# A hand-ordered attention-and-gated-MLP kernel: one written order of all steps replaced by another

## The chip, the cores and the metric

The kernel runs on one core of a Trainium2 chip. The time is the device time of one execution in microseconds (us). The core has five engines with a queue each: TensorE (PE, matrix products), VectorE (DVE), ScalarE (ACT), GpSimd (POOL) and SyncE (SP, which here issues every DMA).

## The reference

Inputs are q, k, v (4 batches, 8 heads, 768 positions, 64 wide), 8 memory keys and values per head, and five weights of an MLP.

```python
for c in range(24):                      # chunks of 32 positions
    k_ctx = k[:, :, max(0, 32*c-16) : min(768, 32*c+40)]   # v_ctx likewise
    scores = q_c @ concat(mem_k, k_ctx).T / 8
    out_c = softmax(scores) @ concat(mem_v, v_ctx)
x = out as (4, 768, 512)
h = gelu_tanh(x @ w_in)                  # 1024 wide
u, v = h[..., :512], h[..., 512:]
v_n = (v - mean(v)) / sqrt(var(v) + 1e-6) * g_ln
v_s = einsum('ts,bsd->btd', w_sg, v_n) + b_sg
result = x + (u * v_s) @ w_out
```

## The kernel before, in words

The kernel holds every operand of the MLP products as a high and a low part, and each product is three products (low x high, high x low, high x high) accumulated in PSUM. All work is cut into some 1230 named steps. The text `ORDER` (line 35) lists the names; the loop at line 565 walks through it and emits each step into its engine's queue. Every engine works its own queue strictly in that order, so `ORDER` is the schedule. A star after a name takes the second engine that the step may use. Buffers are handed out by `Slots` in the order of the text: four PSUM tiles (mma to mmd), two tiles `g` for the gelu of the v half, seven tiles `u`.

The steps, with u for a unit of 128 positions (24 units, six to each batch b), tt for a unit in its batch, h for a half batch (384 positions), j for a group of 128 columns:

- `r`, `d1` to `d6` with `i13` and so on: one 128x512 piece of w_in arrives as 64-bit words (512 KB) and is split into high and low. `r` loads (SP), `d1` ACT (star POOL), `d2` DVE (star ACT), `d3` and `d4` DVE, `d5` ACT, `d6` POOL (star DVE). `ri10` to `ri13` are the four pieces for the v half, `ri00` to `ri03` those for the u half; `ro0` to `ro3` the same for w_out, through one staging tile.
- `g`, `ga`, `gb`: one 128x384 piece of w_sg is loaded into a `u` tile (SP, 192 KB), its high part written by ACT, its low part by POOL (star DVE). Twelve pieces; those that end in 0 serve half 0.
- `q`, `k`, `v` and a unit: loads of 256, 368 and 512 KB (SP).
- Attention of a unit: `S` scores (PE), `mx` maxima and `sb` subtraction (DVE), `ex` exponentials (ACT), `z` clears missing keys (POOL, first and last unit of a batch), `sm` sums and `sr` reciprocals (DVE), `nm` scaling (DVE, star POOL). For units 0 to 9 `T` transposes on PE and `p` copies back (ACT, star DVE); later pairs of units use `yt` (DVE) and four exchanges `Ea` to `Ed` of four small DMAs each. `A` multiplies by the values (PE), `xc` and `xh` copy out and round (ACT), `xl` makes the low part (POOL, star DVE; units 0, 2, 4, 5 always DVE).
- `V` and b, tt: the product with the v half of w_in (PE, 12 matmuls of 512 columns). `v1` to `v4` gelu (ACT, DVE, ACT, DVE), `v5`, `vx` statistics (DVE), `vy`, `v6` the inverse deviation (POOL), `v7` normalization (DVE, star POOL), `v8` high part (ACT), `v9` low part (POOL, star DVE) into the tiles `vh`.
- `U` and b, h, j: the product with the u half (12 matmuls of 384 columns), `u1` to `u4` gelu (ACT, DVE, ACT, DVE).
- `W`: the product of the six `vh` with w_sg (18 matmuls of 384 columns), `w1` scale and shift and `w2` gate (DVE), `w3` high (ACT), `w4` low (POOL, star DVE).
- `O`: the product with w_out (12 matmuls), `o1` adds x (DVE), `out` stores (SP).
- `zz` and a number: so many products of a cleared tile into the first free PSUM tile (function `warm`), whose results nobody reads.

A DMA that loads into a buffer waits on SP until the buffer's last reader is done, and all later DMAs wait behind it. q and k have two buffers each, v three.

The queues in words up to the first `W` of batch 0. SP before: ri13 k0 ri10 g40 g01 q0 g50 g21 g31 ri12 q1 k1 ri11 v0 ri02 q2 ri01 k2 v1 g20 q3 k3 ri00 v2 cb q4 k4 v3 ri03 v4 q5 g41 k5 ro0 and so on. PE before: zz25 S0 zz15 S1 zz3 T0 zz4 A0 zz2 T1 zz5 S2 V00 A1 S3 T2 V01 A2 S4 T3 V02 A3 T4 S5 A4 V03 V04 U003 T5 U000 S6 A5 U002 V05 U012 T6 S7 A6 U010 S8 U011 U001 T7 S9 U013 A7 S10 W011.

Of the kernel before, what the change touches and what calls it, by code (L numbers as in the profile page):

```python
# [40 lines left out]
g41 d3i00 p2 k5 sb3 cbh v500 ex3 vx00 sm3 ro0 A2 v101 sr3 vy00 d4i00 S4 v201 nm3* xh2 v5 d5i00 xl2 q6 v600 xc2  # L41
T3 mx4 d6i00 V02 v301 sb4 k6 p3 d1i03 v401 v700* ex4 v501 sm4 A3 vx01 sr4 d2i03 v800 nm4 xc3 v6 v900* T4 xh3
d3i03 S5 p4 xl3* vy01 v102 v601 A4 mx5 q7 v701* d2o0* k7 v202 V03 xh4 v7 sb5 xc4 xl4 ex5 d3o0 v801 d4i03 v302
v901* d5i03 V04 v402 z5 v103 d6i03 sm5 v203 ga50 sr5 v502 v303 nm5* U003 ga21 v403 ga40 gb21 vx02 ga31 v503
ga20 vx03 vy02 ga01 g30 gb50* T5 ga41 gb20* U000 g11 p5 gb41* g00 gb01* u1003 gb40* g10 u2003 vy03 g51 v602 S6
u3003 gb31 ga30 A5 u4003 q8 ga11 mx6 k8 v702* u1000 U002 v8 sb6 xh5 xc5 u2000 ex6 xl5 v603 ga00 u3000 gb11*
V05 v802 v703 u1002 u4000 z6 v902 ga10 sm6 ga51 u2002 v803 gb10 sr6 v104 U012 u3002 v204 nm6* u4002 v304 v903*
T6 v404 gb00 v105 S7 p6 v504 gb51 u1012 A6 v205 q9 k9 mx7 v305 U010 v9 vx04 xc6 u2012 vy04 v604 v405 u3012
v704* sb7 u4012 ex7 S8 v505 u1010 sm7 U011 k10 v804 q10 u2010 sr7 v904 vx05 u3010 mx8 u4010 U001 nm7 d1o0 sb8
vy05 u1011 ro1 v605 u2011 ex8 v705 u3011 T7 sm8 v805 S9 p7* v905 U013 u4011 k11 mx9 q11 sr8 sb9 d1o1 nm8 A7  # L50
ex9 d4o0 sm9 d2o1* S10 v10 gb30* xc7 sr9 W011 d5o0 d3o1 q12 k12 u1001 mx10 ro2 d4o1 u2001 d5o1 sb10 u3001
d6o1* ex10 W002 w1011 sm10 w2011 sr10 u4001 w3011 d6o0* S11 d2o2* w4011* w1002 d1o2 W000 q13 d3o2 u1013 k13
mx11 ro3 u2013 w2002 u3013 d4o2 w3002 u4013 d5o2 W003 w4002* w1000 d6o2* w2000 w3000 d2o3 w4000 W012 w1003
w2003 d1o3* w3003 d3o3 W010 w4003 w1012 w2012 d4o3 w3012 w4012 d5o3 d6o3 T8 w1010 W013 p8 w2010 nm9 w3010
w4010 sb11 ex11 z11 T9 sm11 A8 p9 nm10* w1013 sr11 w2013 S12 xc8 v11 yt10 w3013 A9 q14 mx12 nm11* k14 sb12
W001 v12 w4013 yt11 ex12 Ec5 z12 sm12 sr12 nm12 O012 w1001 Eb5 w2001 w3001 w4001* S13 o1012 Ea5 O002 mx13 sb13
ex13 q15 O013 sm13 out012 o1002 Ed5 sr13 S14 o1013 O011 mx14 k16 out002 sb14 out013 q16 ex14 k15 O003 sm14
o1011 yt12 out011 sr14 nm13* O001 o1003 out003 yt13 nm14 O000 o1001 out001 S15 o1000 xh6 xh7 out000 O010 xl6
mx15 q17 xh8 xl7* k17 sb15 xl8* ex15 V10 o1010 sm15 out010 xc9 sr15 xh9 xl9* U100 v110 v210 v310 U103 v410
u1100 u2100 v510 u3100 u4100 V13 u1103 vx10 vy10 u2103 v610 u3103 v710 u4103 v810 v910* U101 v113 v213 v313  # L60
V12 v413 u1101 u2101 v513 u3101 u4101 vx13 vy13 V11 v613 v112 v713 v212 v813 v312 v913 v412 A10 v512 v111 v211
S16 xc10 v13 vx12 v311 A11 vy12 mx16 q18 v612 xh10 k18 v411 U102 xc11 Ec6 xl10* xh11 v511 v712 sb16 v812 V14
v14 vx11 u1102 xl11* v912 Ed6 ex16 u2102 sm16 u3102 vy11 v611 u4102 sr16 v711* V15 v114 Ea6 v214 v314 v811
v414 Eb6 S17 v911 v514 vx14 U110 mx17 vy14 v115 v614 v215 k19 v714 v315 q19 U113 v814 v415 u1110 v914 v515
u2110 vx15 U111 u3110 yt14 vy15 v615 u1113 u4110 nm15 u2113 A12 sb17 u1111 u3113 v715 ex17 S18 u4113 v15 v815
u2111 z17 U112 k20 xc12 mx18 q20 u3111 v915* yt15 sm17 W110 nm16 sr17 sb18 u4111 ex18 z18 sm18 S19 w1110 sr18
A13 mx19 k21 q21 w2110 W111 xc13 Eb7 w3110 w4110 u1112 Ea7 u2112 W100 u3112 w1111 u4112 w2111 v16 w3111 Ed7
w4111 W113 w1100 w2100 Ec7 w3100 w4100* W112 w1113 w2113 w3113 w4113* W103 w1112 yt16 w2112 nm17 w3112 w4112*
sb19 W102 w1103 ex19 yt17 w2103 nm18* sm19 w3103 sr19 w4103 S20 w1102 w2102 A14 q22 mx20 k22 w3102 W101 sb20
w4102 xc14 v17 ex20 sm20 sr20 O110 w1101 w2101 w3101 w4101 O111 o1110 out110 O103 o1111 out111 O102 o1103  # L70
out103 O100 o1102 out102 O112 o1100 out100 A15 o1112 out112 S21 Ec8 O101 mx21 k23 v18 O113 o1101 xh12 Ea8 xh14
xl12* xh13 xl14 xl13* V20 o1113 out101 Eb8 U201 v120 v220 out113 xc15 Ed8 v320 V22 xh15 v420 u1201 xl15* u2201
q23 v520 u3201 u4201 V21 v122 vx20 vy20 v222 v620 v720* v322 yt18 v422 V23 v522 v820 nm19 vx22 v920* yt19 vy22
v121 v622 U200 sb21 v722* v221 ex21 v321 sm21 A16 v421 u1200 v822 nm20 S22 u2200 xc16 v19 v922* u3200 A17 xh16
v521 v123 u4200 xl16 U202 Ed9 xc17 vx21 v223 xh17 mx22 vy21 v323 v621 sr21 sb22 xl17 V24 v423 u1202 Eb9 ex22
u2202 v721 u3202 sm22 v821 u4202 v921 Ea9 sr22 V25 v523 vx23 vy23 v124 v623 v224 v723 v20 v324 Ec9 U213 v823
v424 v923 v524 vx24 U211 vy24 v125 v624 u1213 v225 v724* u2213 v325 u3213 U210 v425 u1211 u4213 v824 yt20 v924
v525 A18 u1210 u2211 u2210 nm21* u3211 S23 vx25 v21 xc18 u4211 u3210 vy25 yt21 A19 v625 mx23 U212 xc19 Ec10
nm22 sb23 v725 ex23 u4210 v825 z23 U203 sm23 Ea10 u1212 v925 u2212 sr23 u3212 u4212 W203 Eb10 v22 W213 w1203
Ed10 W202 w1213 w2213 w3213 w4213* yt22 u1203 A20 u2203 nm23* w1202 u3203 w2202 W211 xc20 v23 yt23 w3202 u4203  # L80
w4202* w2203 w3203 w4203 A21 w1211 w2211 W212 Eb11 w3211 w4211* Ea11 W200 w1212 w2212 w3212 Ec11 w4212* W201
w1200 w2200 Ed11 w3200 w4200* W210 w1201 w2201 w3201 w4201 O200 w1210 w2210 w3210 w4210 O201 o1200 out200 O213
o1201 out201 O212 o1213 out213 O211 o1212 out212 O203 o1211 out211 O202 o1203 out203 O210 o1202 xh18 xh20
out202 xl18* xh19 xl20 V30 o1210 xl19 out210 xc21 xh21 V31 v130 xl21* v230 v330 v430 V33 v131 v530 v231 vx30
v331 vy30 v630 v431 U302 v730* v531 vx31 A22 vy31 v830 v631 u1302 v930* U301 xc22 u2302 v731* v133 u3302 v233
xh22 u4302 v333 A23 xl22* v831 v433 u1301 V32 xc23 v931* xh23 u2301 v533 u3301 xl23* u4301 vx33 U312 v132 vy33
v633 v232 v733 v332 V35 v833 v432 u1312 v933 v532 u2312 vx32 u3312 vy32 v632 u4312 V34 v135 v732* v235 v335
v435 v832 U303 v535 v932 vx35 vy35 v134 v635 U310 v234 u1303 v735* u2303 v334 u3303 v434 U311 u4303 u1310 v534
v835 u2310 v935* u3310 U313 vx34 u1311 u4310 vy34 v634 u2311 v734 u3311 v834 u4311 U300 u1313 v934 u2313 u3313
u4313 W313 W301 w1313 w2313 w3313 w4313* u1300 u2300 W311 w1301 u3300 w2301 u4300 w3301 w4301* W312 w1311  # L90
# [543 lines left out]
```

## Time and profile before

| | us |
|---|---|
| median of 3 runs (lowest, highest) | 390.04 (387.78, 390.69) |
| the profiled execution, its own time | 390.77 |
| its span, first to last instruction | 388.7 |
| busy: PE, DVE, ACT, POOL | 375.4, 259.5, 157.0, 127.3 |

All times of the trace are counted from the span's start. PE's busy time includes the `zz` products. The granted clock is TensorE's, as a share of 2.4 GHz.

### The profile page before, as it was taken

How to read it: one execution, taken by the hardware profiler on the slowest of the kernel's cores; microseconds unless marked ns; L12 is line 12 of the kernel's file. 1: busy time of each engine (PE TensorE's matmuls, PEld its weight loads, DVE VectorE, ACT ScalarE, POOL GpSimd, SP SyncE). 2: the span in 40 equal slices, each digit the busy share in tenths (PEclk: the TensorE clock that was granted, in tenths of full speed). 3: DMA queues.
4: the chain of work that ended last, by engine and by line, in shares of the span. 5: the costliest groups of instructions: out<-in, count | busy, mean ns of one | idle time of the engine just before them, and what ended most of it. 6: DMA issues, size and time to landing. Idle time of an engine off the chain costs nothing.

```text
span 388.7 us, 11100 instructions
## 1 busy us (share of the span) xinstructions
PE 375.4 (97%) x4798; PEld 345.5 (89%) x4798; DVE 259.5 (67%) x476; ACT 157.0 (40%) x291; POOL 127.3 (33%) x142
## 2 busy tenths in 40 slices
...
GB/s 289 398 387 288 239 142 123 240 218 147 1 201 131 262 1 57 162 166 119 95 102 84 121 135 77 70 110 95 73 39 81 83 0 2 3 0 2 0 81 83
DMA packets 24529, 47.65 MB, mean 123 GB/s; under 512 B 4384, under 2 KB 13600, under 8 KB 24480
## 3 DMA queue, kind: packets, MB, share of 16 engines
...
q14 instruction: 11, 0.09, 0.1%
HBM read 36.96 MB, written 6.29 MB: 111 GB/s over the span
## 4 chain that ended last, share of the span: by engine, by line
PE 74%; DVE 10%; SPq 4%; DMA 4%; ACT 3%; issue 2%; POOL 2%; DVEq 0%; POOLq 0%; ACTq 0%
PE mma L105 18%; PE mmd L105 17%; PE mmb L105 16%; PE mmc L105 14%; PE av L105 5%; SPq L105 4%; PE s L105 3%; DMA ka<-in_ks 2%; DMA kb<-in_ks 1%; DMA pt<-y 1%; DVE na L105 1%; DVE w_sg_lo L105 1%; DVE ga L105 1%; ACT ea L105 1%; DVE rdc L105 1%
## 5 line engine op out<-in xcount | busy, mean ns | idle before, releaser
L105 DVE SCALAR_TENSOR_TENSOR mmd<-mmd,g_half,b_half 128x384 f32<-128x384 f32 x11 | 6.9, 624 | 14.4 <-PE mmd L105 14.4
L105 PE MATMUL mma<-vhf 128*128 128x512 f32 x43 | 13.4, 474 | 2.3 <-POOL vhf L105 2.3
L105 PEld LDWEIGHTS mma<-vhf 128*128 128x128 f32 x43 | 9.8, 235 | 4.8 <-POOL vhf L105 2.3
L105 POOL TENSOR_SCALAR rsa<-mva 128x1 f32<-128x1 f32 x8 | 2.0, 248 | 36.0 <-DVE mva L105 36.0
L105 PE MATMUL mmc<-w_in_hi,paira 128*128 128x512 f32 x48 | 13.4, 401 | 0.1
L105 DVE STREAM_TRANSPOSE y<-na 128x512 f32<-128x512 f32 x14 | 9.9, 707 | 3.8 <-DMA pt<-y 2.9
L105 ACT ACTIVATE ea<-ea 128x512 f32<-128x512 f32 x12 | 7.6, 635 | 11.1 <-DVE ea L105 11.0
L105 ACT ACTIVATE eb<-eb 128x512 f32<-128x512 f32 x12 | 7.6, 635 | 11.1 <-DVE eb L105 11.0
L105 PEld LDWEIGHTS s<-kb,qb 64*32 64x32 f32 x768 | 8.4, 105 | 3.8 <-DVE xa L105 1.8
L105 PE MATMUL s<-kb,qb 64*32 64x64 f32 x768 | 10.3, 224 | 1.5 <-DMA kb<-in_ks 1.5
L105 DVE SCALAR_TENSOR_TENSOR gb<-gb,mma 128x512 f32<-128x512 f32 x10 | 6.9, 686 | 6.9 <-ACT gb L105 6.9
L105 PE MATMUL s<-ka,qa 64*32 64x64 f32 x768 | 10.3, 224 | 0.7 <-DVE eb L105 0.7
L105 PEld LDWEIGHTS av<-pt,va 64*64 64x64 f32 x512 | 8.3, 134 | 2.9 <-ACT pt L105 1.4
L105 PEld LDWEIGHTS s<-ka,qa 64*32 64x32 f32 x768 | 8.4, 105 | 2.7 <-issue 1.1
L105 PEld LDWEIGHTS mmc<-w_in_hi,paira 128*128 128x128 f32 x48 | 8.7, 188 | 2.1 <-DVE paira L105 0.3
L105 PEld LDWEIGHTS av<-pt,vc 64*64 64x64 f32 x512 | 8.5, 134 | 2.3 <-issue 0.9
L105 PE MATMUL av<-pt,vc 64*64 64x32 f32 x512 | 9.4, 221 | 0.7 <-ACT xc L105 0.7
L105 PEld LDWEIGHTS av<-pt,vb 64*64 64x64 f32 x512 | 8.4, 134 | 1.8 <-issue 1.1
L105 PE MATMUL av<-pt,va 64*64 64x32 f32 x512 | 9.2, 220 | 0.8 <-ACT pt L105 0.8
L105 ACT ACTIVATE ga<-ga 128x512 f32<-128x512 f32 x12 | 7.6, 634 | 5.6 <-DVE ga L105 5.5
L105 DVE SCALAR_TENSOR_TENSOR ga<-ga,mmc 128x512 f32<-128x512 f32 x12 | 8.2, 681 | 2.3 <-ACT ga L105 2.3
L105 DVE SCALAR_TENSOR_TENSOR mma<-mma,g_half,b_half 128x384 f32<-128x384 f32 x7 | 4.4, 625 | 7.5 <-PE mma L105 7.5
(535 smaller groups left out, 1249.7 us busy)
## 6 DMA issues: line engine op xcount, KB each, us to landing
...
pt<-y SPq DMA_DIRECT2D x112, 32.0 KB, 2.3
...
```

The costliest lines, as they stand in the source:

```text
L105: return self.tc.keep_in_program_order(getattr(self.engine, name)(*args, **kw))
```

## The change

Only the text `ORDER` changes. It holds the same steps as before, in another order; 85 of them change their engine (among those on DVE before and POOL now: `nm1`, `nm2`, `nm7`, `nm9`, `nm17`, `nm19`, `nm22`; from POOL to DVE `nm0`, `nm10`, `nm21`, `nm23`). DVE gets 464 steps in place of 476, ACT 295 for 290, POOL 138 for 131. The `zz` products go from 54 to 39 and stand at other places. Below are the old text up to the first `W` and the new text up to there and at the places that the prediction names.

```diff
-ri13 k0 ri10 g40 g01 q0 g50 g21 d2i13* d1i13* g31 ri12 d3i13 d4i13 d2i10* q1 d1i10* d5i13 k1 ri11 d3i10 zz25
-S0 v0 d6i13* ri02 d4i10 q2 mx0 d5i10 ri01 sb0 d6i10 ex0 k2 d2i12* z0 sm0 d1i12 v1 d3i12 zz15 S1 g20 sr0 d4i12
-nm0* mx1 d5i12 q3 d1i11 sb1 zz3 T0 d2i11 ex1 d6i12* p0 sm1 zz4 A0 k3 d3i11 sr1 d4i11 d1i02 ri00 nm1 xc0 v2
-d2i02 zz2 T1 xh0 d3i02 d5i11 xl0 cb d2i01* d6i11 d1i01 zz5 S2 p1 d3i01 V00 mx2 q4 k4 d4i01 sb2 v3 d5i01 d4i02
-ex2 d6i01 d5i02 sm2 A1 v100 sr2 ri03 nm2 S3 xc1 v200 d6i02 xh1 T2 v4 mx3 v300 xl1* d2i00* q5 v400 d1i00 V01
...
+ri13 d2i13 d1i13 d3i13 d4i13 d5i13 zz4 zz6 zz2 q0 k0 d6i13 ri12 S0 zz13 zz3 zz7 mx0 sb0 ri10 d2i12* d1i12
+d3i12 d4i12 ex0 z0 d2i10* ri11 d5i12 d1i10 d2i11* d1i11 sm0 d3i10 sr0 nm0 T0 k1 q1 S1 v0 d4i10 d3i11 d6i12*
+d4i11 q2 k2 ri01 k3 q3 ri00 v1 mx1 sb1 p0 d5i10 A0 d5i11 xh0 ex1 xl0 d6i11* d6i10 S2 sm1 sr1 mx2 sb2 V00
+d2i01* d1i01 ex2 d3i01 d4i01 sm2 S3 mx3 sr2 nm1* T1 nm2* sb3 v100 xc0 v200 d2i00* p1 zz3 A1 T2 zz1 d3i00 v2
+ri02 ex3 v300 xc1 xh1 d1i00 p2 sm3 sr3 v400 v500 vx00 nm3* T3 A2 d2i02* vy00 v600 xl1* d4i00 V01 xc2 d1i02
+v700 v800 xh2 p3 d3i02 d4i02 xl2 v101 k4 v3 q4 cb ri03 v4 d5i00 v201 v900 cbh d6i00 S4 k5 q5 k6 g11 g10 g40 q6
+g21 A3 V02 mx4 sb4 d5i02 d6i02* d2i03* v301 v401 v501 xc3 xh3 d5i01 d1i03 xl3* d3i03 vx01 d4i03 S5 V03 g30 q7
+mx5 d6i01* sb5 S6 d5i03 d6i03 U001 v102 ex4 v202 sm4 v302 ga10 ga30 vy01 v601 gb10 sr4 nm4 T4 v402 v701 mx6
+sb6 ga40 ga11 ga21 p4 u1001 gb40 gb21 v801 ex6 ex5 z6 z5 v502 vx02 u2001 sm5 U002 k7 S7 A4 ro0 g20 g50 g51 k8
+g31 q9 q8 v5 k9 v6 d2o0* u3001 u4001 gb11 xh4 u1002 ga20 xc4 mx7 sr5 xl4 v901 nm5* vy02 u2002 v103 v203 sm6
+sr6 u3002 ga50 gb20 v602 U003 u4002 sb7 v702 V04 ga31 u1003 v303 u2003 v403 v503 T5 p5 v802 S8 mx8 vx03 nm6*
+A5 ga51 ex7 xh5 xl5 sm7 sr7 gb30* sb8 v902 T6 U000 xc5 p6 u3003 u1000 v104 V05 vy03 gb50* gb31 nm7* v603 gb51
+k10 v7 u4003 ex8 v204 v304 sm8 v703 v404 S9 A6 T7 v504 sr8 mx9 g41 g00 v803 ga41 p7 gb41* u2000 nm8 vx04 q10
+v903 g01 v105 ga00 ga01 vy04 q11 k11 v8 U012 U011 u3000 xc6 v205 sb9 ex9 sm9 u4000 u1011 v305 v405 u2011 S10
+mx10 v505 A7 vx05 v604 v704* gb01 gb00 T8 p8 v804 xc7 u3011 U013 U010 vy05 v605 v705 u1012 v805 u1010 v905
+d1o0 v904* A8 sb10 u4011 S11 d3o0 u2012 u2010 u3010 W001 u3012 sr9 u4010 nm9* mx11 u4012 W002 W003 sb11 d4o0
...
+nm15 sb17 o1012 xh9 xh10 xh11 v811 xl9* q18 out011 S18 v13 out013 k20 vy10 xl10* mx18 xl11* yt15 V13 out010
...
+V15 U112 V14 xc12 v115 v215 v315 vy13 v613 v713 u1112 u1110 v415 v515 vx15 v813 vy15 u2112 u2110 v913* ex18
+v114 v214 v314 A13 S19 mx19 v414 v514 vx14 v615 v715* v815 u3112 u4112 U111 u1111 xc13 u3110 z18 v915* vy14
+v614 U113 U100 v714 u4110 u1113 v814 v914* u2113 u3113 u4113 W110 w1110 u2111 u3111 w2110 Ed7 q20 k21 Ea7 Ec7
...
+U203 v19 v18 Eb9 out111 out113 Ea9 Ec9 k23 q23 out110 Ed9 vy23 v623 sr21 v422 u2200 u2201 u3200 u3201 v522
+v723* v823 v923 u1203 xl17* u4201 mx22 u2203 vx22 vy22 v622 v722* V24 v124 u3203 u4200 v224 u4203 v324 v424
+sb22 v524 vx24 U213 V25 U210 U212 A18 v822 v922* vy24 v624 v724* v125 v225 v325 v425 u1213 v525 yt20 u2213
...
+out301 out211 out212 out210 o1300 o1313 out312 out313 out300 O310 o1310 out310 O302 o1302 out302
```

## Rows read from the trace of the kernel before

**Rows 1.** The page: busy us, share of the span, instructions, by engine.
```profile
PE 375.4 (97%) x4798; PEld 345.5 (89%) x4798; DVE 259.5 (67%) x476; ACT 157.0 (40%) x291; POOL 127.3 (33%) x142
```

**Rows 2.** Windows: us, length, busy PE, PEld, DVE, ACT, POOL, PE clock, DMA share, GB/s.
```profile
0.00:10.00 10.00, 7.65 (x22) 6.04 (x23) 2.69 (x5) 3.14 (x4) 4.77 (x12) 1.00 0.82 293
...
20.00:30.00 10.00, 8.82 (x226) 6.56 (x219) 9.71 (x15) 6.75 (x13) 5.67 (x5) 1.00 1.05 388
...
11.87:85.59 73.72, 69.07 (x1401) 57.73 (x1402) 68.29 (x125) 51.15 (x97) 41.21 (x39) 0.98 0.71 249
...
82.10:385.30 303.20, 300.30 (x3334) 283.89 (x3328) 190.90 (x354) 104.71 (x195) 80.74 (x91) 1.00 0.28 87
```

**Rows 3.** PE in order of time, 0 to 83 us: start, length, tile, [idle before].
```profile
2.35 8.70 PE L105 MATMUL mma<-vhf 128*128 128x512 f32 x25 [2.35 <-POOL vhf L105]
10.98 0.86 PE L105 MATMUL s<-ka,qa 64*32 64x64 f32 x64
...
23.80 1.20 PE L105 MATMUL mmc<-w_in_hi,paira 128*128 128x512 f32 x4
...
31.18 1.31 PE L105 MATMUL mma<-w_in_hi,paira 128*128 128x512 f32 x4 [1.14 <-DVE paira L105]
...
35.70 1.14 PE L105 MATMUL av<-pt,vc 64*64 64x32 f32 x64
36.77 0.86 PE L105 MATMUL s<-ka,qa 64*32 64x64 f32 x64
37.55 0.66 PE L105 MATMUL mmb<-ident,na 128*128 128x128 f32 x4
...
48.22 1.09 PE L105 MATMUL mma<-w_in_hi,pairb 128*128 128x512 f32 x4
...
51.02 0.86 PE L105 MATMUL mmd<-paira,w_in_lo 128*128 128x384 f32 x4
...
53.11 0.60 PE L105 MATMUL mmc<-ident,na 128*128 128x128 f32 x4
53.46 0.94 PE L105 MATMUL mmb<-paira,w_in_lo 128*128 128x384 f32 x4
...
82.10 0.44 PE L105 MATMUL mmb<-w_sg_hi,vha 128*128 128x384 f32 x1
```

**Rows 4.** Windows of PE alone: us, length, busy PE, clock, DMA share, GB/s.
```profile
2.35:5.00 2.65, 2.65 (x6) 1.00 0.96 376
...
8.00:10.00 2.00, 2.00 (x10) 1.00 1.07 390
...
33.00:34.00 1.00, 1.00 (x4) 0.50 1.05 408
```

**Rows 5.** DVE in order of time.
```profile
11.87 0.69 DVE L105 TENSOR_REDUCE mxa<-s 128x8 f32<-128x512 f32 x1 [1.28 <-PE s L105]
...
22.19 0.68 DVE L105 TENSOR_TENSOR paira<-av,paira 128x512 fp32r<-128x512 f32 x1
...
27.55 1.78 DVE L105 TENSOR_TENSOR na<-ea,rdc 128x512 f32<-128x512 f32 x1
```

**Rows 6.** DMA issues on SP, 0 to 32 us, and in us to landing, rawc and y.
```profile
5.69 0.46 SPq L105 DMA_DIRECT2D rawc<-in_w_in  x1
...
DMA to landing us min/median/max: 6.8/6.8/6.8
...
31.07 0.43 SPq L105 DMA_DIRECT2D y<-in_w_out  x1
...
DMA to landing us min/median/max: 6.4/6.4/6.4
```

**Rows 7.** PE in order of time after 82 us: the longest idle time.
```profile
130.77 0.85 PE L105 MATMUL s<-kb,qb 64*32 64x64 f32 x64 [1.46 <-DMA kb<-in_ks]
```

**Rows 8.** POOL in order of time.
```profile
15.81 1.44 POOL L105 TENSOR_TENSOR na<-ea,rda 128x512 f32<-128x512 f32 x1 [1.59 <-DVE rda L105]
```

More of the change, by code (lines that the diff above doesn't have):

```diff
@@ L41 @@
[L41 to L90, printed above, removed]
@@ new lines @@
+k10 v7 u4003 ex8 v204 v304 sm8 v703 v404 S9 A6 T7 v504 sr8 mx9 g41 g00 v803 ga41 p7 gb41* u2000 nm8 vx04 q10
+v903 g01 v105 ga00 ga01 vy04 q11 k11 v8 U012 U011 u3000 xc6 v205 sb9 ex9 sm9 u4000 u1011 v305 v405 u2011 S10
+mx10 v505 A7 vx05 v604 v704* gb01 gb00 T8 p8 v804 xc7 u3011 U013 U010 vy05 v605 v705 u1012 v805 u1010 v905
+d1o0 v904* A8 sb10 u4011 S11 d3o0 u2012 u2010 u3010 W001 u3012 sr9 u4010 nm9* mx11 u4012 W002 W003 sb11 d4o0
+d5o0 ex10 w1001 w2001 w3001 ro1 d2o1* k12 v10 d1o1 d3o1 d4o1 d5o1 k13 v9 q13 q12 ex11 w1002 w4001 w2002 w1003
```

36 lines of the change are left out of this document (33 added, 3 removed).

## The prediction

> **What bounds the kernel now.** The page's first part comes first: PE is busy 97% of the span [rows 1], so time can only come from PE's own work or from stretches where PE idles, waits or spends itself on products that nobody reads. The windows show where these are. From 82.10 us to the last product PE idles 303.20 - 300.30 = 2.90 us in all [rows 2], 1.46 of it in front of one score product [rows 7]. Ahead of 82.10 the picture is another one. By then PE has done 11 S, 8 A, 8 T, 6 V and 8 U, in the order of the text. One S takes 0.78 us from its start to the next start, A 1.07, T 0.35, V 2.80, U 2.09 [rows 3]: 8.6 + 8.6 + 2.8 + 16.8 + 16.7 = 53.5 us. So 28 of the first 82 us are not needed by PE. In the first 10 us VectorE works 2.69 us, because it waits for data; from 11.87 (the first maximum, [rows 5]) to 85.59 (the first `w1`, right behind the first W) it is busy 68.29 of 73.72 us with 125 instructions, 93% [rows 2]. The DMA engines are full too in that time (share 1.05 at 20 to 30 us, [rows 2]). The start is bound by loads in the order in which SP issues them, and then by VectorE's queue; after 82 us PE bounds.
>
> **The loads.** SP's DMAs land in the order of issue, at one pace: rawc (`ri12`) lands at 5.69 + 6.8 = 12.5 us and y (`ro0`) at 31.07 + 6.4 = 37.5 [rows 6]. In the old SP queue 3,120 KB are issued up to and with `ri12`, 12,642 KB up to and with `ro0` (512 KB for r and v, 368 for k, 256 for q, 192 for g, 386 for `cb`). That is 9,522 KB in 25.0 us, 381 KB per us, and a byte count of X lands at 4.3 + X/381. The new queue puts the w_sg pieces, five of which stand before `ri12` now, behind `k6`, and moves q0 ahead of k0. Its counts: k0 1,136, ri12 1,648, ri10 2,160, ri11 2,672, q1 3,296, v0 3,808, k2 4,432, v1 6,592, v2 7,104. So they land at 7.3, 8.6, 10.0, 11.3, 13.0, 14.3, 15.9, 21.6 and 22.9; by the same rule the old ri11 (4,256) landed at 15.5 and v0 (4,768) at 16.8.
>
> **The warm-up products.** Of 54 there remain 39, 12 of them before S0 in place of 25. The first ones run at the lower clock level, 6 in 2.65 us or 0.44 each, those from 8 us on at the higher one, 10 in 2.0 us [rows 4] (the clock column reads 1.00 in both; I go by the pace). Twelve end at 2.35 + 12 x 0.43 = 7.5 us, when k0 is there, and S0 starts at 7.5 in place of 10.98 [rows 3]. The other 23 before T0 fill 8.4 to 13.4 at 0.22 each, inside the wait for `nm0`; they cost nothing unless T0 is ready sooner. The last 4 stand in waits as well.
>
> **To the first V.** I walk down VectorE's new queue, 0.60 us from one 512-wide instruction to the next and 0.70 where a result is waited for (one takes 0.69, [rows 5]): mx0 8.45, sb0, d3i12, d4i12, sm0 to 11.8, d3i10, sr0, nm0 to 13.2. `nm0` now runs on VectorE for 0.6 us in place of 1.44 on POOL, where it ended at 17.25 [rows 8]. T0 is at 13.3, p0 behind it, A0 at 14.5 (v0 landed at 14.3) until 15.5. VectorE goes on with d4i10, d3i11, d6i12, d4i11, mx1, sb1 to 16.9; ACT writes xh0 until 16.7, so xl0 ends at 17.5 (now 22.87, [rows 5]) and d6i11 at 18.1. V00 starts near 18.0; it starts at 23.80 now [rows 3]. **Gain at this point: 5.8 us.**
>
> **To the first W.** Two counts. The first walks down PE: from V00 to W001 stand 6 V, 8 U, 9 S, 8 A, 8 T, 16.8 + 16.7 + 7.0 + 8.6 + 2.8 = 51.9 us, 0.9 us of warm-ups and some 2.5 us where PE changes kind. With waits of about 1.2 in all around T1, T3 and A2 this gives 74.5. The second walks down VectorE: the new queue has 120 instructions between mx0 and `w1001`; at the present mean, 73.72/125 = 0.590 us with its idle time in it, w1001 comes at 8.45 + 70.8 = 79.2, so W001 starts 3.2 us before, at 76.0. The later of the two holds: 76.0. At that point the new order has done one S, one A and one T more than the old one at 82.10, so the point to compare is 82.10 + 2.2 = 84.3. **Gain: 8.3 us.** The w_sg pieces have become urgent in return: `g41`, `g00`, `g01` wait for `u` tiles that `gb50`, `gb31`, `gb51` free at 56 to 59.5 us, land by 64, and ACT splits them in front of `u3000`, `xc6` and `v305`; by my walk v905 ends at 73.5, 1 us before W001 is due. That cover is thin.
>
> **After the first W.** The same PE work remains, at the same pace, so 300.3 us of it stay. The present 2.90 us of idle could go; against it stand three places where I find a margin under 1 us: W110 (`V14`'s normalization has 8.1 us between V14 and W110), A18 (16 exchange DMAs and five more issues of 0.3 to 0.6 us each in 15 us), W311. I credit nothing. `out211`, `out212`, `out210` move behind `out301`: 11 stores in the last 10 us of PE, 192 KB or 0.5 us each at the pace above, so they still fit; exposed, they would cost 1 us. VectorE's 12 instructions fewer give nothing here, where it is idle a third of the time.
>
> **The sum.** 390.77 (the profiled execution) - 8.3 = 382.5. The median of the three runs is 390.04, 0.7 lower, so the forecast for a median is **381.7 us**, 2.1% faster. Its own bounds: 377.3, if the PE walk holds (9.9) and the 2.9 us go as well; 386, if W001 comes 4 us later than 76.
>
> **Rivals.** (1) *POOL and VectorE get in each other's way.* `nm1` to `nm3` stand on POOL in the densest stretch. One `na` on VectorE took 1.78 us where 0.69 is usual, at 27.55 us [rows 5], while POOL was at work. If each of the three costs VectorE 1.1 us: 381.7 + 3.3 = 385.0. Against it: in all POOL has hardly more to do before W (41 steps for 40, and three fewer of its longest, `v7`). The Trainium skill, SBUF — State Buffer, section Who interferes with whom, says that a VectorE instruction with two SBUF inputs contends with a GpSimd instruction that reads SBUF, and that the one issued second blocks until the first is done; the 1.78 us agree, and by that rule the moved `nm` are where the time would go.
>
> (2) *The clock falls more often.* Now V01 runs its products at 0.50 [rows 4], behind a wait of 1.14 us, and takes 35.70 - 31.18 = 4.52 us against V04's 2.80 [rows 3]: 1.7 us. The new order has 15 fillers less and between V00 (ends 20.4) and V01 (28.3) only 5 us of PE work. The forecast takes one such fall again. With two more: 381.7 + 3.4 = 385.1; then the fillers don't do what they are put there for. The Trainium skill, TensorE: Matmul & The Clock Gate, section Why this matters for your kernels, says to leave no long idle gaps of PE between bursts; by it the fewer fillers speak against the change, and the trace agrees as far as one fall goes.
>
> (3) *The early start is not kept.* VectorE may need 0.65 us for each of the 120 instructions: 0.06 x 120 = 7.2 us more to W001, 389 us, no change. For it: VectorE is the second bound and the new queue issues its steps earlier than the data of some of them. Against it: the 0.590 us already hold the waits of a queue that is as crowded, and the new one has fewer steps in it.
>
> (4) *Slower: ACT held by the late w_sg pieces.* ACT works in order; if `ga01` waits for its DMA, `u3000`, `xc6`, `ex9` and `v305` wait behind it, and v405 to v905 follow, 9 us from `ga01` to the end of v905. W001 is then at `g01`'s landing + 10. At 64 it is harmless; at 74.3 the whole gain is gone; from 78 on the kernel is slower by over 1%, at 80 it is 390.04 + 5.7 = 395.7. That needs `gb51` on POOL, and with it the load behind it, 14 to 16 us late. A load takes up to 6.8 us to land [rows 6], so two such loads in a row, each waiting for the tile that the other frees, would make it.
>
> **Chances.** Forecast 0.52; better than it, near 377.3, 0.10; rivals 1 and 2, 0.18 together; rival 3 0.11; rival 4 0.09. A measurement of this kernel tells 1% from no change, 3.9 us. Faster by over 1% (under 386.1): 0.52 + 0.10 + 0.18 = 0.80; within 1%: 0.11; slower: 0.09. The range leaves out rival 4, the worse half of rival 3 and a little below the better case: 377.0 to 388.5.
>
> **What would show it.** Right: S0 near 7.5 us, T0 near 13.3, V00 near 18, V01 near 28, U001 near 40, W001 near 76 without an idle time in front of it, and still under 4 us of PE idle behind it. Wrong: V00 on time but W001 after 80 (rivals 1, 3, 4: rows over 1 us on VectorE for 1, ACT's rows of w_sg_hi released by a DMA for 4); several windows of granted clock 0.50 before 60 us (2); new waits of A10, A12, A18 for pt, or of W110 and W311 for vh.

## The result, and the profile of the kernel after

After: 386.99 us median (383.91 to 389.13, 20 runs), before in the same series 390.66 (387.78 to 394.82, 20 runs): ratio 0.9901, 95% interval 0.9876 to 0.9926. The change saves 3.7 us, 1.0%, where the forecast had 2.1%. The profiled execution took 386.81 us, span 385.0. Medians of before differ a little from series to series below (390.2 to 390.8), so ratios are compared.

PE's row of the page, as [rows 1], first column the busy time:

```profile
PE 372.0 (97%) x4783; PEld 343.6 (89%) x4783; DVE 251.8 (65%) x464; ACT 155.3 (40%) x296; POOL 128.1 (33%) x149
```

PE in order of time up to the first W, as [rows 3]:

```profile
2.35 5.46 PE L105 MATMUL mma<-vhf 128*128 128x512 f32 x12 [2.35 <-POOL vhf L105]
7.76 0.85 PE L105 MATMUL s<-ka,qa 64*32 64x64 f32 x64
...
13.90 0.60 PE L105 MATMUL mma<-ident,na 128*128 128x128 f32 x4
...
18.07 1.20 PE L105 MATMUL mmb<-w_in_hi,paira 128*128 128x512 f32 x4
...
23.92 1.14 PE L105 MATMUL av<-pt,vb 64*64 64x32 f32 x64 [0.70 <-DMA vb<-in_vs]
...
27.25 0.66 PE L105 MATMUL mma<-ident,na 128*128 128x128 f32 x4 [1.38 <-POOL na L105]
...
28.90 1.20 PE L105 MATMUL mmc<-w_in_hi,paira 128*128 128x512 f32 x4
...
33.81 1.01 PE L105 MATMUL av<-pt,va 64*64 64x32 f32 x53 [0.71 <-issue]
...
39.07 0.24 PE L105 MATMUL s<-kb,qb 64*32 64x64 f32 x1 [0.50 <-issue]
...
43.02 0.97 PE L105 MATMUL mma<-paira,w_in_lo 128*128 128x384 f32 x4
...
79.07 0.45 PE L105 MATMUL mmc<-w_sg_hi,vha 128*128 128x384 f32 x1
```

Read against [rows 3]: S0 at 7.76 (10.98), V00 at 18.07 (23.80), V01 at 28.90 (31.18), the first W at 79.07 where 84.3 is the point to compare. So 5.7 us are gained at V00, and 5.2 at W: 84.3 - 79.07.

The end, though, is only 4.0 us earlier (the last O starts at 378.95; in the trace of before it starts at 382.99). So 1.2 us go behind W. PE there, 126 to 137 us; the number in brackets is the idle time before the row:

```profile
126.30 1.55 PE L105 MATMUL mma<-pairb,w_out_hi 128*128 128x384 f32 x8
128.77 1.44 PE L105 MATMUL av<-pt,vb 64*64 64x32 f32 x64 [0.92 <-ACT xa L105]
130.59 1.18 PE L105 MATMUL s<-ka,qa 64*32 64x64 f32 x64 [0.38 <-DVE eb L105]
131.71 1.93 PE L105 MATMUL av<-pt,vc 64*64 64x32 f32 x64
133.57 1.65 PE L105 MATMUL mmd<-paira,w_in_lo 128*128 128x384 f32 x4
135.01 2.64 PE L105 MATMUL mmd<-paira,w_in_hi 128*128 128x384 f32 x8
...
137.49 0.86 PE L105 MATMUL mmb<-w_in_hi,paira 128*128 128x512 f32 x3
```

The windows of the same stretch (columns as [rows 2]; the eighth number is the granted clock):

```profile
128.00:130.00 2.00, 1.23 (x64) 1.20 (x64) 1.51 (x5) 1.08 (x2) 1.74 (x3) 1.00 0.00 0
130.00:132.00 2.00, 1.62 (x89) 1.34 (x85) 1.30 (x3) 1.22 (x2) 1.89 (x2) 0.63 0.03 8
132.00:134.00 2.00, 2.00 (x65) 1.94 (x59) 2.00 (x5) 1.47 (x3) 1.27 (x2) 0.50 0.53 160
...
136.00:138.00 2.00, 2.00 (x9) 1.91 (x8) 1.12 (x3) 0.32 (x1) 0.80 (x2) 0.66 0.23 56
```

A10 and S16 wait, PE idles 0.77 of the 2 us from 128, the granted clock falls to 0.50 until about 137, and the products run at half pace: U102's last eight take 2.64 us where the O before them took 1.55 for eight of the same shape. From the row at 126.30 to the first product of V10 (137.49) it takes 11.19 us; in exchange_early below, without wait and half clock, the same steps take 6.78 (127.78 to 134.56). So 4.4 us are lost here, in this execution. The wait of S15 [rows 7] is gone in return. What A10 waits for is on ACT and SP. First ACT's row, then SP's queue:

```profile
128.13 0.59 ACT L105 COPY xa<-av 128x512 f32<-128x512 f32 x1 [4.26 <-DMA out<-xa]
```

```profile
118.88 0.38 SPq L105 DMA_DIRECT2D qb<-in_qs  x1
119.30 0.43 SPq L105 DMA_DIRECT2D kb<-in_ks  x1
119.77 2.42 SPq L105 DMA_DIRECT2D pt<-y  x4
122.23 0.58 SPq L105 DMA_DIRECT2D ka<-in_ks  x1
123.08 0.68 SPq L105 DMA_DIRECT2D out<-xa  x1
```

`xc9` writes `xa`, which the store `out003` must have read first; that store is issued at 123.08, behind two v loads, q17, k17, the four DMAs of the exchange `Ec5` and k16, and lands at 128. The exchange itself lands at 127, and from it `yt12`, `nm13`, `yt13` and `sb15` follow one after the other to S16.

### The profile page after: what moved, and what is told of

Same layout as the page of the kernel before. It is cut to its first block, busy times and chain, and to the rows that moved or that the text cites. A ratio compares the mean times of both kernels' runs of the same rounds, so it can differ in the third digit from the quotient of the medians.

```text
span 385.0 us, 11079 instructions
## 1 busy us (share of the span) xinstructions
PE 372.0 (97%) x4783; PEld 343.6 (89%) x4783; DVE 251.8 (65%) x464; ACT 155.3 (40%) x296; POOL 128.1 (33%) x149
## 4 chain that ended last, share of the span: by engine, by line
PE 82%; DMA 5%; DVE 4%; SPq 4%; issue 2%; ACT 1%; POOL 1%; DVEq 0%; POOLq 0%; ACTq 0%
PE mmd L105 21%; PE mmb L105 19%; PE mma L105 19%; PE mmc L105 14%; PE av L105 6%; SPq L105 4%; PE s L105 4%; DMA rawc<-in_w_in 2%; DMA vb<-in_vs 2%; DMA pt<-y 1%; POOL na L105 1%; DVE rda L105 0%; DVE y L105 0%; DVE eb L105 0%; DVE rdb L105 0%
## 5 line engine op out<-in xcount | busy, mean ns | idle before, releaser
L105 POOL TENSOR_TENSOR paira<-ug,paira 128x384 fp32r<-128x384 f32 x4 | 4.1, 1016 | 39.7 <-ACT paira L105 39.7
L105 DVE STREAM_TRANSPOSE y<-na 128x512 f32<-128x512 f32 x14 | 9.8, 702 | 6.9 <-DMA pt<-y 3.9
L105 PE MATMUL mma<-vhf 128*128 128x512 f32 x36 | 11.5, 479 | 2.4 <-POOL vhf L105 2.4
L105 DVE SCALAR_TENSOR_TENSOR mmd<-mmd,g_half,b_half 128x384 f32<-128x384 f32 x12 | 7.4, 620 | 8.8 <-PE mmd L105 8.8
L105 DVE SCALAR_TENSOR_TENSOR mmb<-mmb,g_half,b_half 128x384 f32<-128x384 f32 x8 | 5.0, 625 | 11.9 <-PE mmb L105 11.9
L105 PEld LDWEIGHTS av<-pt,vb 64*64 64x64 f32 x512 | 8.6, 134 | 4.0 <-issue 1.4
L105 PEld LDWEIGHTS s<-ka,qa 64*32 64x32 f32 x768 | 8.6, 109 | 3.9 <-issue 1.7
L105 PEld LDWEIGHTS mma<-vhf 128*128 128x128 f32 x36 | 8.2, 234 | 4.3 <-POOL vhf L105 2.4
L105 PE MATMUL s<-ka,qa 64*32 64x64 f32 x768 | 10.6, 231 | 1.3 <-DVE eb L105 1.3
L105 PE MATMUL av<-pt,vb 64*64 64x32 f32 x512 | 9.5, 220 | 2.1 <-DMA vb<-in_vs 1.2
L105 PEld LDWEIGHTS s<-kb,qb 64*32 64x32 f32 x768 | 8.5, 105 | 3.2 <-issue 2.7
L105 PEld LDWEIGHTS av<-pt,vc 64*64 64x64 f32 x512 | 9.1, 145 | 2.4 <-issue 2.3
L105 DVE SCALAR_TENSOR_TENSOR gb<-gb,mmb 128x512 f32<-128x512 f32 x10 | 6.8, 677 | 6.7 <-ACT gb L105 6.6
L105 PE MATMUL mmb<-w_in_hi,paira 128*128 128x512 f32 x40 | 11.1, 399 | 0.0
L105 PE MATMUL s<-kb,qb 64*32 64x64 f32 x768 | 10.6, 224 | 0.5 <-issue 0.5
L105 POOL TENSOR_TENSOR na<-eb,rdb 128x512 f32<-128x512 f32 x4 | 4.3, 1074 | 19.0 <-DVE y L105 15.4
L105 DVE SCALAR_TENSOR_TENSOR mma<-mma,g_half,b_half 128x384 f32<-128x384 f32 x8 | 5.0, 623 | 8.5 <-PE mma L105 8.4
L105 PE MATMUL av<-pt,vc 64*64 64x32 f32 x512 | 10.1, 230 | 0.4 <-issue 0.4
L105 PEld LDWEIGHTS av<-pt,va 64*64 64x64 f32 x512 | 8.5, 134 | 2.2 <-issue 1.8
L105 PE MATMUL av<-pt,va 64*64 64x32 f32 x512 | 9.5, 221 | 0.7 <-issue 0.7
L105 ACT ACTIVATE ga<-ga 128x512 f32<-128x512 f32 x12 | 7.6, 633 | 5.2 <-DVE ga L105 5.1
L105 ACT ACTIVATE eb<-eb 128x512 f32<-128x512 f32 x12 | 7.6, 630 | 5.3 <-DVE eb L105 5.3
```

Source lines behind the costliest of these rows:

```text
L105: return self.tc.keep_in_program_order(getattr(self.engine, name)(*args, **kw))
```

## The experiments

Fifteen kernels, each the order of before or of after with a few names moved. Two theories recur. A: the gain is made ahead of the first W and kept by whatever follows. D: what the later stages wait for is a DMA that stands late in SP's queue, the exchange `Ec5` first of all. Other letters stand beside what they say. In most of these kernels the order text has four lines fewer, so L101 is L105.

**Halves of the change.** The first kernel has the new order up to W001 and takes all other steps in the order of before; the second the reverse.

```diff
@@ new_start_old_rest, behind W001 @@
-u3012 sr9 u4010 nm9* mx11 u4012 W002 W003 sb11 d4o0
+v9 u3012 u4012 u4010 ro1 d1o1 d4o0 d2o1* v10 sr9 W011 d5o0 d3o1 q12 k12
...
```

> The new order up to the first W (W001, 79.07 us in the new kernel's trace), then all remaining steps in the old order with their old engines. Theory A (the new start gains what the traces show, 84.3 - 79.07 = 5.3 us, and the new rest gives part of it back): about 390.7 - 5.3 = 385.4 us, ratio 0.986, better than the new kernel's 0.990. Theory B (the start gains nothing that lasts; the rest is what made the kernel faster): ratio 0.997 or more. The places where the old rest waited (S15, S18, A17) may move.

Measured: 391.61 us, ratio 1.0034 (1.0004 to 1.0065).

```diff
@@ old_start_new_rest, behind S10 v10 gb30* xc7 sr9 @@
-W011 d5o0 d3o1 q12 k12 u1001 mx10 ro2 d4o1 u2001 d5o1 sb10
+u1001 u2001 u3001 u4001 mx10 T8 p8 A8 sb10 S11 W001 nm9* mx11 W002 W003 sb11
...
```

> The old order up to its first W (W011, 82.1 us), then the remaining steps in the new order with their new engines. Theory A: no gain of the start, and the new rest's own wait at A10 and S16 with the clock's fall, 4.5 us, less the old rest's 2.9 us of idle that goes: ratio 1.000 to 1.005. Theory B: about 0.990, as the new kernel.

Measured: 393.78 us, ratio 1.0085 (1.0054 to 1.0116). Both halves alone are slower than before, by 0.3% and 0.9%. By its number the first falls to theory B, the second to neither. In the first the start is early (first W at 80.80, where 84.3 is the point to compare), but S15 starts at 130.48, nearly as in [rows 7]. That doesn't show that the halves pay only together: old_order_late_gates below keeps an early start through the whole old order. A half is a third order, whose queues need not fit at the seam (in the second, A8 waits 1.47 us for `pt` just behind it); that this is what the early start was lost to is argued, not shown.

**The stall at A10 to S16.** The first kernel moves the store alone, the second the exchange too.

```diff
-out002 v11 v12 q17 k17 Ec5 k16 out003
@@ out003_early @@
+out002 out003 v11 v12 q17 k17 Ec5 k16
@@ exchange_early @@
+out002 Ec5 out003 v11 v12 q17 k17 k16
```

> The new order with the store out003 moved ahead of v11, v12, q17, k17, the exchange Ec5 and k16. Theory C (the copy xc9, which must wait until that store has read its buffer, holds A10 at 128 us, and that wait makes the clock fall): A10 starts at 127.9 in place of 128.8, the clock does not fall, 3 to 4.5 us faster than the new kernel, ratio 0.979 to 0.982. Theory D (the late exchange of units 10 and 11 holds yt12, nm13, yt13, sb15 and with them S16 at 130.6): A10 0.9 us earlier but S16 no earlier, the clock falls all the same, ratio 0.990 within 0.2%.

Measured: 387.42 us, ratio 0.9921 (0.9887 to 0.9955): no gain on the change. In its trace A10 no longer waits, but S16 does, for `sb15` (first W at 80.94, so all stands 1.9 us later than in the change):

```profile
132.68 0.86 PE L101 MATMUL s<-ka,qa 64*32 64x64 f32 x64 [1.87 <-DVE eb L101]
```

One part of theory D did not come: the clock did not fall here (1.00 from 124 to 138 us). From the O to V10 it takes 8.60 us (128.12 to 136.72).

> As the run before, and the last exchange of units 10 and 11 (Ec5) also moved ahead of the loads v11, v12, q17, k17. Theory D: the exchange lands near 122.5 us in place of 127.0, yt12, nm13, yt13 and sb15 follow 4 us earlier, neither A10 nor S16 waits, the clock stays at 1.00, 4 to 4.5 us faster than the new kernel: ratio 0.979. Theory C: no more than the run before. If both are wrong and the v11 and v12 loads, now 2.4 us later, hold A11 or A12, no gain.

Measured: 384.26 us, ratio 0.9854 (0.9816 to 0.9893). PE in exchange_early at the same steps:

```profile
127.78 1.55 PE L101 MATMUL mma<-pairb,w_out_hi 128*128 128x384 f32 x8
129.26 1.21 PE L101 MATMUL av<-pt,vb 64*64 64x32 f32 x64
130.52 0.85 PE L101 MATMUL s<-ka,qa 64*32 64x64 f32 x64
131.29 1.14 PE L101 MATMUL av<-pt,vc 64*64 64x32 f32 x64
...
134.56 1.08 PE L101 MATMUL mmb<-w_in_hi,paira 128*128 128x512 f32 x4
```

No wait, no half pace, and U102 follows at 132.36 in place of 133.57, although this execution reached W001 1.5 us later (80.60). From W001 to the last O it took 295.3 us, the change 299.9. So of the 4.4 us some 1.8 are the wait for the exchange (8.60 against 6.78) and some 2.6 the half clock that followed the waits in the execution of the change. Theory D holds for the wait: the exchange, not the store, sets this place, and the place of one block of four DMAs is worth 3.2 us against out003_early in the same series (2.6 by the ratios; some 2 us against the change, whose interval it just touches, as it does that of out003_early).

**More and fewer warm-up products.** exchange_fill is exchange_early with fuller waits; no_fill is the change without its two small runs behind A1 and T2; no_warmup has none at all.

```diff
-A0 d5i11 ... p1 zz3 A1 T2 zz1 d3i00
@@ exchange_fill @@
+A0 zz4 d5i11 ... p1 zz7 A1 T2 zz7 d3i00
@@ no_fill @@
+A0 d5i11 ... p1 A1 T2 d3i00
```

> exchange_early with more warm-up products in the waits ahead of V01: 4 behind A0, 7 in place of 3 behind T1, 7 in place of 1 behind T2 (49 in all). Theory F (the clock falls between 26 and 35 us in many executions of the new start, as in the traces of new_start_old_rest, out003_early and exchange_early, and each fall costs V01 1.4 to 1.9 us): no window at 0.50 before 60 us, V01 takes 3.0, W001 near 79 in place of 80.6, ratio about 0.981. Rival: the products run past the arrival of nm3 and hold T3, or the falls don't matter because VectorE's queue is late anyway: W001 no earlier than 80.5, ratio 0.985 or more.

Measured: 384.05 us, ratio 0.9829 (0.9809 to 0.9849), mean granted clock 0.998 to 1.000 in all four executions (53 products, not the 49 of the expectation). W001 is at 78.36, as theory F has it, but the gain on exchange_early (0.9854) lies within the intervals.

> The new order without the 4 warm-up products inside the waits behind T1 and T2. Theory F: with PE less busy ahead of V01 the clock falls in this stretch, one or two windows, V01 near 4.5 us, W001 1.5 to 3 us later than without a fall: ratio 0.993 to 0.997. If four products are too few to matter: ratio 0.990, clock as in the new kernel or with one fall at the same place.

Measured: 386.44 us, ratio 0.9880 (0.9847 to 0.9912), not told apart from the change.

> The changed kernel without any warm-up product (all zz removed); nothing else differs. Theory W (the products hold the granted clock up while the loads come): the granted clock is 0.50 in several stretches between 8 and 40 us, the small products of S0 to V00 take longer, W001 starts at 83 us or later instead of 79.07, and the time is 390 to 393. Rival L (loads and VectorE set the start, the products only fill waits): S0, T0, V00 stand within 0.7 us of 7.8, 13.9 and 18.1, W001 at 79 to 81, the time 386 to 388.

Measured: 386.94 us, ratio 0.9916 (0.9885 to 0.9947). Its windows, in the same columns:

```profile
26.00:28.00 2.00, 0.61 (x8) 0.38 (x4) 1.93 (x5) 1.97 (x5) 0.79 (x1) 0.88 0.94 324
28.00:30.00 2.00, 1.69 (x28) 1.36 (x32) 1.68 (x4) 1.00 (x2) 1.54 (x3) 0.50 0.79 240
30.00:32.00 2.00, 1.93 (x50) 1.73 (x46) 1.15 (x2) 0.30 (x1) 0.14 (x1) 0.50 1.01 399
32.00:34.00 2.00, 2.00 (x6) 1.52 (x6) 0.82 (x2) 2.00 (x5) 0.56 (x1) 0.50 0.91 362
```

PE is idle for most of 26 to 28 and then runs at half pace, yet the first W comes at 80.69, 1.6 us behind the change, and the time is the same within its interval. S0 starts at 6.85, when its data lands, 0.9 us ahead of the change. Rival L holds: the `zz` products of the new order are worth at most the 2 us that these intervals leave. The Trainium skill, TensorE: Matmul & The Clock Gate, section Why this matters for your kernels, asks for no long idle gaps between bursts; these rows agree that a gap is followed by the lower clock, and show how little it can cost where PE waits for others anyway.

**v1 ahead of k3.** SP issued nothing from 9.9 to 15.3 us, since `k3` waits for S1, and v1 stood behind it; A1 then waited 0.70 us for `vb`. The edit is made on exchange_early.

```diff
-k2 ri01 k3 q3 ri00 v1
+k2 ri01 v1 ri00 k3 q3
```

> exchange_early with the loads v1 and ri00 moved ahead of k3, whose issue waits for S1 and in the new kernel holds the whole queue from 9.9 to 15.3 us. Theory G (the blocked queue makes the values of unit 1 late, 23.9 us where my count of bytes gave 21.6): A1 no longer waits for vb, starts near 23.2, and V01 and W001 follow up to 0.7 us earlier, ratio 0.983 to 0.985. Rival H (T3 behind nm3, and with it VectorE and POOL, decide when V01 starts): A1 earlier, V01 and W001 as before, ratio 0.985 as exchange_early.

Measured: 386.85 us, ratio 0.9881 (0.9850 to 0.9912). Its executions spread from 383.43 to 391.83, and no gain shows. In its trace A1 starts without a wait (23.45), but T3 then waits 1.83 us for POOL, and V00 to V01 takes 11.24 us, in the change 10.83: A1's wait for `vb` is not where the missing microseconds are. This kernel has the exchange early too and is not told apart from the change; whether the move of v1 costs what the exchange gains, or the six executions scatter, the run doesn't decide.

**nm1 to nm3 back on VectorE.**

```diff
-nm1* T1 nm2* ... nm3* T3
+nm1 T1 nm2 ... nm3 T3
```

> The new order with nm1, nm2 and nm3 on VectorE instead of POOL, all else as it is. My rival 1 of the prediction (POOL and VectorE get in each other's way): each of the three saves up to 1.1 us on VectorE and adds 0.6, T3 is 0.5 us earlier, ratio 0.987. VectorE as the bound of the start: three times 0.6 us more in its queue, W001 1.8 us later, ratio 0.9945. If neither bounds: 0.990 within 0.2%.

Measured: 390.58 us, ratio 0.9978 (0.9948 to 1.0008), 3 us worse than the change. PE at T3:

```profile
29.49 1.11 PE L101 MATMUL mma<-ident,na 128*128 128x128 f32 x4 [2.86 <-DVE na L101]
```

T3 waits 2.86 us for VectorE where it waited 1.38 for POOL. Behind that wait the clock falls (0.50 from 29.4 to 36.2 us, where the trace of the change has no fall), so the 3 us need not be VectorE's alone. In the change a VectorE instruction that takes 0.69 us elsewhere starts beside one of POOL and takes 1.79:

```profile
34.57 1.79 DVE L105 TENSOR_TENSOR w_in_lo<-ma,w_in_hi 128x512 fp32r<-128x512 f32 x1
34.52 1.29 POOL L105 TENSOR_TENSOR w_in_lo<-me,w_in_hi 128x512 fp32r<-128x512 f32 x1
```

So the two do get in each other's way, as the Trainium skill, SBUF — State Buffer, section Who interferes with whom, says; three instructions off the fuller queue are still the better bargain.

**The old order with the loads of the new.** Nothing of the compute steps is touched: the six w_sg pieces go behind k5, and the first warm-up run is cut from 25 products to 14. Both edits, then each alone, then one more load.

```diff
-ri13 k0 ri10 g40 g01 q0 g50 g21 d2i13* d1i13* g31 ri12 ... zz25 S0 ... S1 g20 ... k5
+ri13 k0 ri10 q0 d2i13* d1i13* ri12 ... zz14 S0 ... S1 ... k5 g40 g01 g50 g21 g31 g20
@@ old_order_late_gates_k15 has this too @@
-S13 o1012 Ea5 ... q16 ex14 k15
+S13 k15 o1012 Ea5 ... q16 ex14
```

> The order of before with only the loads rearranged as the change does: the six early w_sgT tiles (g40 g01 g50 g21 g31 g20) behind k5, and the first warm-up run cut from 25 products to 14, so that S0 can start when its data lands. Theory P (the gain at the start is that of the loads): S0 at 8.5 or less, V00 at 20 to 21 instead of 23.80, W001 at 81 to 82 instead of 84.3, time 387.5 to 388.5. Theory Q (VectorE's order sets the start, loads alone only shift the wait): S0 early, but V01 within 1 us of 31.2, W001 at 83.5 or later, time 389.5 to 391.

Measured: 386.97 us, ratio 0.9932 (0.9903 to 0.9961), the whole change's time. PE in its trace:

```profile
2.35 5.07 PE L101 MATMUL mma<-vhf 128*128 128x512 f32 x14 [2.35 <-POOL vhf L101]
7.61 0.85 PE L101 MATMUL s<-ka,qa 64*32 64x64 f32 x64 [0.18 <-DMA qa<-in_qs]
...
21.05 1.19 PE L101 MATMUL mmc<-w_in_hi,paira 128*128 128x512 f32 x4
...
28.43 1.20 PE L101 MATMUL mma<-w_in_hi,paira 128*128 128x512 f32 x4 [1.14 <-DVE paira L101]
...
33.32 0.66 PE L101 MATMUL mmb<-ident,na 128*128 128x128 f32 x4
...
78.31 0.44 PE L101 MATMUL mmb<-w_sg_hi,vha 128*128 128x384 f32 x1
```

Theory P holds in the time. S0 is 3.4 us earlier than in [rows 3], V00 and V01 2.75 each, with the wait of 1.14 us before V01 unchanged: the old chain moved as a block. The first W is 3.8 earlier (78.31 against 82.10); part of that is the clock, which in this execution doesn't fall in V01 (V01 to T3 takes 4.89 us, in [rows 3] 6.37).

> The order of before with one edit: the first warm-up run is 14 products instead of 25; the loads stand as before. Theory P (the gain of old_order_late_gates is that of the load order): S0 starts when its data is there, W011 stays within 1 us of 82.1 and the time is 389.5 to 390.5. Rival (25 products held TensorE past the landing of S0's data): W011 at 79 to 80, time 387 to 388.

Measured: 388.79 us, ratio 0.9955 (0.9933 to 0.9978), between the two expectations: the cut alone gains 1.7 us. S0 at 8.94, now waiting for its own load, W011 at 80.08:

```profile
8.94 0.85 PE L101 MATMUL s<-ka,qa 64*32 64x64 f32 x64 [1.68 <-DMA qa<-in_qs]
```

> The order of before with only the six w_sgT tiles moved behind k5; the first warm-up run keeps its 25 products. Theory P: VectorE gets its first tiles earlier, S0 stays at 10.98 since the products hold TensorE, W011 at 79.5 to 81, time 387.5 to 389. Rival (the loads alone are worth nothing while TensorE is held): W011 at 82, time 390.

Measured: 390.79 us, ratio 1.0006 (0.9979 to 1.0032). PE:

```profile
2.35 8.55 PE L101 MATMUL mma<-vhf 128*128 128x512 f32 x25 [2.35 <-POOL vhf L101]
10.83 0.86 PE L101 MATMUL s<-ka,qa 64*32 64x64 f32 x64
```

Here my expectation missed and its rival came true: with 25 products ahead of it S0 can't use its early data, and 82.09 for W011 is the old time. The two edits belong together: the products held TensorE, and behind them the load of q0. How much the loads add to the cut is seen in S0 (7.61 against 8.94); the intervals of the two times overlap. Neither the loads nor the products show as a wait of PE in the trace of before, where S0's row [rows 3] carries no bracket at all.

> old_order_late_gates with one more load moved: k15 stands right behind S13 in the order, ahead of the exchanges Ea5 and Ed5, instead of behind q16. Theory D (what ends the waits of the middle is a load late in SP's queue): S15, which waited 1.8 us for kb there (1.46 us before), starts without a wait, and the time is 1.3 to 1.8 us under old_order_late_gates: 385.2 to 385.7, ratio 0.987. Rival: S15 then waits for VectorE's eb (sb15) or the stage after it takes the gain back, and the time stays at 386.5 to 387.

Measured: 387.64 us, ratio 0.9924 (0.9893 to 0.9954). S15's wait for `kb` is gone (127.67, right behind the O), but the time is not better: here theory D missed. Its profile shows two long waits with no releaser:

```profile
43.01 0.32 PE L101 MATMUL s<-kb,qb 64*32 64x64 f32 x9 [2.11 <-issue]
...
151.73 0.91 PE L101 MATMUL av<-pt,vc 64*64 64x32 f32 x49 [1.30 <-issue]
```

The first stands far ahead of the edit, in PE steps that old_order_late_gates has too, where it took 0.86 us: it is no work of the edit.

**Fillers in the old order**, in the waits ahead of V01:

```diff
-S3 ... T2 v4
+S3 zz3 ... T2 zz7 v4
```

> The order of before with only two more warm-up runs: 3 products behind S3 and 7 behind T2, in the waits of 28 to 32 us ahead of V01. Theory C (the half clock of V01 is a loss of its own): no stretch at 0.50 between 28 and 38 us, V01 takes 3.0 us instead of 4.52, W001 starts about 1.5 us earlier, time 389.0, ratio 0.996. Rival: VectorE's queue, not the products, sets what follows V01, and W001 stays within 0.4 us of 84.3, time 390 to 391; or the fillers run over into V01 and it is slower, 391 to 392.

Measured: 390.55 us, ratio 0.9999 (0.9970 to 1.0027). PE:

```profile
30.98 1.10 PE L101 MATMUL mma<-w_in_hi,paira 128*128 128x512 f32 x4
...
33.87 1.14 PE L101 MATMUL av<-pt,vc 64*64 64x32 f32 x64
...
37.45 0.32 PE L101 MATMUL s<-ka,qa 64*32 64x64 f32 x9 [1.74 <-issue]
37.70 0.66 PE L101 MATMUL mmb<-ident,na 128*128 128x128 f32 x4
```

V01 takes 2.89 us at full clock in place of 4.52, A2 starts 1.8 us earlier (0.9 of it from an earlier start of this execution, V00 at 22.90), and S4 then waits 1.74 us without a releaser: T3 is at 37.70, in [rows 3] at 37.55. In this execution the time of the half clock was waited for a step later; in old_order_late_gates, where the clock didn't fall either, no such wait stood there. The fillers held the clock at 0.998 or more in only 5 of the 12 executions. What the fall costs in the old order is better read from the kernel before itself: in the series of these experiments 53 of its executions have a mean clock of 0.996, as the profiled one with its one fall, and take 390.5 us in the median, 17 have 0.999 to 1.000 and take 390.3.

**The best of these**: exchange_fill, with v22 ahead of the exchange `Ea11`.

```diff
-Ea11 out201 Ec11 Eb11 out203 v23 out200 out202 out213 v22
+v22 Ea11 out201 Ec11 Eb11 out203 v23 out200 out202 out213
```

> exchange_fill with one more move: the load v22 stands ahead of the exchange Ea11 in SP's queue instead of behind out213. Theory D (a transfer that stands late in SP's queue is what the tail of a stage waits for): A22, which waited 0.5 us for vb in the changed kernel and about 1 us in exchange_fill, starts without a wait, U302 has its nominal length, and the time is 0.5 to 1.0 us under exchange_fill: 383.0 to 383.6, ratio to the kernel before 0.981. Rival: A22 finds its next wait at the same place (ACT xa or pt), and the time stays at 384.0.

Measured: 383.31 us, ratio 0.9813 (0.9776 to 0.9851); A22 starts without a wait (306.86), but the step is too small to tell from exchange_fill. Both beat the kernel before by 1.7 to 1.9%, and the intervals of both lie below the change's.

## Why the prediction was right or wrong

The direction was right, the range, widened for the rivals, held the time, and the size was twice too large: 8.3 us forecast, 3.7 measured. By the classes of its chances, 386.99 us stands at the edge of "within 1%", which had 0.11. Two slips in its sums weigh nothing: 84.3 - 74.5 is 9.8, not 9.9, and a V of 2.8 us from 18.0 on ends at 20.8, not 20.4. By its steps:

- **The loads.** Right up to v0 (S0 at 7.76, forecast 7.5; A0 at 15.21, forecast 14.5). Wrong for v1, which lands at 23.8, not 21.6: the byte count took SP's queue as never blocked, but `k3` waits for S1. exchange_v1 shows no time in it.
- **The warm-up products.** Right in their times, and too small in their part. I counted the shorter first run as a detail of S0; the three kernels on the old order show that alone it is worth 1.7 us, and together with the w_sg loads behind k5 as much as the whole change.
- **To the first V.** Right: 18.0 forecast, 18.07 measured.
- **To the first W.** The step that failed first: 76.0 forecast, 79.07 measured, so 5.2 us in place of 8.3. Nearly all of the miss lies between V00 and U001 (40 forecast, 43.02 measured); from U001 to W001 it took 36.05 us where the forecast had 36.0. V01 came 0.9 us late; from V01 to U001 stand three V, three S and one A, 12.4 us at 3.0, 0.79 and 1.07 each, which took 14.1 where the forecast had 12.0 in all; 1.7 of it are the stretched A3 (+1.0) and S5 (+0.7), the two with "issue" rows. No row of PE between V01 and U001 waits for another engine, so VectorE's queue, which the forecast took as the bound, did not hold this stretch. The term that was too small is 70.8 us for VectorE's 120 instructions from `mx0` to `w1001`: they took 74.1. Some 0.5 of the 3.3 is the count: the window of before holds 124 whole instructions, its 125th is the first `w1` itself, so the mean was 0.594. They were not slower at work; VectorE idled 8.4 us in that time (5.4 before, [rows 2]), most of it for ACT (4.7) and POOL (2.8). A mean with the old order's idle time in it says nothing of the idle time in a new order. The window, columns as [rows 2]:

```profile
8.65:82.76 74.11, 69.04 (x1532) 59.02 (x1533) 65.72 (x121) 52.26 (x100) 37.90 (x42) 1.00 0.73 253
```

- **After the first W, "I credit nothing".** The step that failed second. I looked for thin margins at W110, A18 and W311, and none of these waits (W110 at 172.53, W311 at 339.42 without a bracket). The margin that was missing was A10's, which I had named only as something to look for, and S16's, which I had not named. There 4.4 us were lost, some 2.6 of them at half clock, so the end lies 1.2 us behind what W001 promised, in spite of the old waits that went. exchange_early took it back.
- **Rival 1** (POOL and VectorE in each other's way): a row of 1.79 us is there, 1.1 more than usual and about what the prediction gave one such row, but PE has no wait for VectorE until 52.47, and nm_on_dve is 3 us slower, so the move to POOL is a gain.
- **Rival 2** (the clock): it falls, once in this trace, at a place that I had not looked at. In the nine traces of the new start with its `nm` on POOL a fall ahead of W goes with a later first W (77.57 to 79.07 without one, 79.37 to 80.94 with one), but the fillers, added or taken away, in the old order or the new, move no median beyond its interval, and some of what W001 gains is waited for later (from W001 to the last O exchange_fill takes 297.6 us, exchange_early 295.3). Over the whole kernel it stays open: of the change's 20 executions the six with the lowest mean clock (0.985 to 0.989) take 388.3 us in the median, the seven with the highest (0.996 to 1.000) 385.7. Whether the falls cost that or only go with longer waits isn't shown.
- **Rival 3** (VectorE needs 0.65 us for each of the 120): about half of it is in the trace, 74.1 us or 0.618 each, 3.3 us of the 7.2 that the rival stood for, and as idle time, not as slower instructions.
- **Rival 4** (ACT held by the late w_sg pieces): didn't happen, the first W has no wait; `g40` and five more behind k5, with the shorter first run, gain in the old order.

So the new order of all steps and engines bought, in time, what six moved loads and eleven products fewer buy in the old order. Its own part was spent in the middle: with the exchange moved, the new order is worth 0.9854 to 0.9813 (0.9881 with v1 moved too), against 0.9932 and 0.9924 for the old order with the new loads. Two things are argued and not shown: that the change's own gain comes from the same two edits (no kernel here puts the early w_sg loads and the 25 products back into the new order), and that the old order has no such place in its middle left to mend.
